# Row tiles 2 and 3 of batch 0 in the first 16 half steps of token block 0, and an earlier place for the next batch's bounds

## The chip, the cores and the metric

The kernel runs on one core of a Trainium2 chip. The metric is device time in microseconds (us), the median of the runs. Of three runs of the kernel before the median is 876.29 us (873.26 to 876.75). One further execution was profiled; every row below is from it.

## What is computed

The reference is a causal attention with a decay, followed by two feed-forward layers; only the core of it is shown.

```python
# q, k, v: 4 batches x 8 heads x 576 x 64, f: 4 x 8 x 576
scores = scale * q @ k.T
cum = cumsum(log(clip(f, 1e-4, 1)))
attn = softmax(where(causal, -1e9, scores + cum[:, None] - cum[None, :]))
x = (attn @ v)                      # as 2304 tokens x 512
h = x @ w_in                        # 512 -> 2048
x = (h * tanh(softplus(h))) @ w_out # 2048 -> 512
h = x @ w2_in                       # 512 -> 1024
s = h * softmax(h)
out = (layernorm(s) * g_ln) @ w2_out
```

## The kernel before, in words

Products run in halves: each operand is a 16-bit high part and a 16-bit low part, and three products (high-high, high-low, low-high) make one.

**Attention.** A batch has five row tiles of 128 query rows (tile 4 of batch 0 has 64), and a tile is worked in steps of 4, 2, 1, 1, 1 heads: 30 steps a batch, 120 in all (`seq`). A step runs through `step_s` (scores on PE into one of three PSUM tiles `sp`), `step_r` (row maximum on DVE, exponential on ACT into one of two buffers `p`), `step_h` (high part by a cast, low part on POOL, both in `ph`, two buffers; every second step of one head a transposing DMA `pT<-ph` leaves, two buffers `pT`), and `step_pv`, three steps behind (products with v on PE). `fin` closes a row tile: it scales the sums on DVE (`x`), splits them (`xh`, low part on POOL) and sends a transposing DMA into `xT`, the input of a token block of 256 tokens. Token block 1 needs row tiles 2 and 3 of batch 0.

**Feed-forward.** For each of nine token blocks, 16 ups (`up`, 12 matmuls each, L786) and 16 downs (`down`, L830) alternate, one of each in two half steps; between them lies the activation (`mish_a`, `mish_b`, `mish_c`, mostly on ACT). Attention steps are dealt to half steps by `att_slots`: `EB` = 190 half steps share the cost of all steps evenly, `lo` makes a block's steps be there by the end of the block before, `hi` holds them back.

**Weights.** While token block 0 runs, `w_in` and `w_out` are loaded in 1 MB parts (`wi_r`, `wo_r`, two buffers), unpacked on DVE (L133, L135, L137), bounded by a small product on PE (`gram`, L156, then `bound`), scaled to a high part on ACT (L198), and given a low part by products on PE (L205, L206) and a copy on ACT (L207).

**The next batch.** `ahead` is called with every step. It loads k and v of the next batch (`load_raw`, three buffers `raw` of 256 KB), squares them on ACT to bound them (`stats`, L330, buffer `x32`, which `fin` uses too), turns the bounds into scales (`scales`), and later loads q, k, v again, tile by tile, and splits them (`split_k`, `split_q`, `split_v`).

**What sets the order.** Every DMA goes out from one queue, SP's, in its order; an entry that waits holds all behind it. A scheduler lays the instructions of each engine out ahead of the run; its order starts from the program's and follows what it believes to be ready. So an edit in `ahead` or `att_slots` moves rows on every engine. A row below that names "issue" or an L number of a helper (L214 and the like) stands in a function called from those named here.

## Time and profile before

| | |
|---|---|
| median of 3 runs | 876.29 us |
| profiled execution, its own time | 874.98 us |
| span of its trace | 873.2 us |
| PE busy | 767.9 us (88%) |
| DVE, ACT, POOL busy | 593.5, 565.7, 392.1 us |
| chain that ended last, by engine | PE 42%, DVE 19%, DMA 16%, ACT 11% |

The time of the profiled execution is 1.8 us longer than its span; times of the trace count from the start of the span. PE is the busiest engine over the whole span; the rows further down show by stretches where it is not.

### The profile page before, as it was taken

What the parts mean: (1) busy time and instruction counts of PE and PEld (TensorE: products, weight loads), DVE (VectorE), ACT (ScalarE), POOL (GpSimd) and SP (SyncE); (2) the same over time, 40 slices, a digit from 0 to 9 for tenths busy, and PEclk for the clock granted to TensorE, in tenths of its full rate; (3) what the DMA queues carried; (4) which work ended last, traced back from release to release, by engine and by line L of the source; (5) the groups of instructions that cost most, each with busy time, mean ns of one, the idle gap of its engine ahead of it and who ended that gap; (6) DMA issues with size and microseconds to landing.
All of it is one profiled execution on the core that took longest, in us unless ns stands there. A gap on an engine that the chain in (4) does not pass through costs nothing.

```text
span 873.2 us, 16633 instructions
## 1 busy us (share of the span) xinstructions
PE 767.9 (88%) x6255; PEld 481.8 (55%) x6255; DVE 593.5 (68%) x1160; ACT 565.7 (65%) x1234; POOL 392.1 (45%) x321
## 2 busy tenths in 40 slices
PE   0469988779999988998889999986999999999997
PEld 0335555566667656566656666653555554444443
DVE  6797862757867989758897764689656454666451
ACT  5747766778768877778867667786965554333331
POOL 2232221645776677755587653226743132012110
PEclk9979999858999999999999999999999999999999
DMA  9998330788999789797897734662112523344453
GB/s 233 243 265 248 125 116 19 135 171 156 155 161 186 141 147 171 167 197 127 165 187 111 134 62 73 168 210 82 25 38 60 97 50 71 86 109 99 106 90 80
DMA packets 328573, 114.90 MB, mean 132 GB/s; under 512 B 317676, under 2 KB 317676, under 8 KB 328492
## 3 DMA queue, kind: packets, MB, share of 16 engines
q1 hardware_dynamic: 328492, 113.84, 63.5%
q8 instruction: 49, 0.80, 0.4%
q14 instruction: 32, 0.26, 0.1%
HBM read 46.59 MB, written 9.55 MB: 64 GB/s over the span
## 4 chain that ended last, share of the span: by engine, by line
PE 42%; DVE 19%; DMA 16%; ACT 11%; issue 6%; POOL 4%; SPq 1%; DVEq 0%; POOLq 0%; ACTq 0%
PE h L1027 10%; PE o L1067 10%; PE x L830 8%; PE h L786 7%; DMA pT<-ph 5%; DVE th L807 2%; POOL ph L518 2%; DVE ph L515 2%; DVE ta L803 2%; DMA wi_r<-in_moe_w_in_dram 2%; DMA rawk<-in_k_dram 1%; PE sp L205 1%; ACT p L479 1%; DMA wo_r<-in_moe_w_out_dram 1%; DMA w2i_r<-in_moe_w_in_dram 1%
## 5 line engine op out<-in xcount | busy, mean ns | idle before, releaser
L830 PE MATMUL x<-wout,gt 128*128 128x512 f16 x864 | 218.6, 386 | 18.6 <-ACT gt L812 8.5
L786 PE MATMUL h<-xT,win 128*128 128x256 f16 x1728 | 216.2, 274 | 1.5 <-DMA xT<-xh 1.5
L786 PEld LDWEIGHTS <-win 128*128 128x128 f16 x1728 | 166.1, 98 | 39.5 <-issue 2.8
L518 POOL TENSOR_TENSOR ph<-p,ph 128x512 f16<-128x512 f32 (+4 forms) x120 | 151.6, 1267 | 79.1 <-ACT ph L517 41.4
L813 POOL TENSOR_TENSOR gt<-th,gt 128x512 f16<-128x512 f32 x72 | 93.9, 1305 | 150.7 <-ACT gt L812 146.7
L830 PEld LDWEIGHTS <-gt 128*128 128x128 f16 x864 | 80.3, 99 | 99.3 <-ACT gt L812 13.5
L1055 POOL TENSOR_TENSOR z<-sl,z 128x1024 f16<-128x1024 f32 x18 | 38.7, 2150 | 138.2 <-DVE s2c L1034 111.3
L1027 PE MATMUL h<-w,x2T 128*128 128x512 f16 x432 | 98.4, 380 | 2.3 <-POOL w L221 1.2
L1067 PE MATMUL o<-wo,zT 128*128 128x512 f16 x432 | 96.5, 379 | 1.0 <-DMA zT<-z 1.0
L807 DVE SCALAR_TENSOR_TENSOR th<-ta,th 128x512 f32<-128x512 f32 x72 | 67.2, 934 | 40.7 <-ACT ta L806 40.4
L549 PE MATMUL pv<-vt,pT 128*128 128x64 f16 (+3 forms) x480 | 72.7, 205 | 23.3 <-DMA pT<-ph 20.1
L479 ACT ACTIVATE p<-sp,nm 64x64 f32<-64x64 f32 (+7 forms) x128 | 61.2, 484 | 34.1 <-DVE nm L477 21.6
L435 PE MATMUL sp<-kt,qa 128*128 128x128 f16 (+3 forms) x480 | 70.4, 221 | 12.8 <-ACT p L479 8.5
L436 PE MATMUL sp<-kt,qb 67*128 67x128 f16 (+3 forms) x480 | 72.1, 222 | 4.4 <-DMA kt<-dd 3.1
L812 ACT CAST gt<-th 128x512 f16<-128x512 f32 x72 | 44.4, 617 | 47.6 <-DVE th L807 46.1
L549 PEld LDWEIGHTS <-pT 128*128 128x128 f16 (+3 forms) x480 | 46.6, 103 | 48.3 <-DMA pT<-ph 31.5
L550 PE MATMUL pv<-vt,pT 128*128 128x64 f16 (+3 forms) x480 | 72.0, 201 | 0.0
L551 PE MATMUL pv<-vt,pT 128*128 128x64 f16 (+3 forms) x480 | 71.9, 201 | 0.0
L1027 PEld LDWEIGHTS <-x2T 128*128 128x128 f16 x432 | 42.3, 98 | 53.0 <-issue 3.1
L1067 PEld LDWEIGHTS <-zT 128*128 128x128 f16 x432 | 42.2, 98 | 52.1 <-DMA zT<-z 1.5
L1038 ACT ACTIVATE e<-h,s2c 128x1024 f32<-128x1024 f32 x18 | 21.7, 1204 | 68.0 <-DVE s2c L1036 68.0
L803 DVE TENSOR_SCALAR ta<-ta 128x512 f32<-128x512 f32 x72 | 49.9, 694 | 22.3 <-ACT ta L798 22.1
(231 smaller groups left out, 1496.8 us busy)
## 6 DMA issues: line engine op xcount, KB each, us to landing
wi_r<-in_moe_w_in_dram SPq DMA_DIRECT2D x8, 1024.0 KB
wo_r<-in_moe_w_out_dram SPq DMA_DIRECT2D x8, 1024.0 KB
rawk<-in_k_dram SPq DMA_DIRECT2D x25, 256.0 KB
rawv<-in_v_dram SPq DMA_DIRECT2D x25, 256.0 KB
x2d<-x2h SPq DMA_DIRECT2D x18, 256.0 KB
out_dram<-ro SPq DMA_DIRECT2D x18, 256.0 KB
w2i_r<-in_moe_w_in_dram SPq DMA_DIRECT2D x4, 1024.0 KB
w2o_r<-in_moe_w_out_dram SPq DMA_DIRECT2D x4, 1024.0 KB
```

The costliest lines, as they stand in the source:

```text
L435: nc.tensor.matmul(o, qa[:, h, r0:r1_], kc[:, h, a0:a1], start=True, stop=False)
L436: nc.tensor.matmul(o, qb_[:67, h, r0:r1_], kc[:67, H + h, a0:a1], start=False, stop=(c != i))
L518: nc.gpsimd.tensor_tensor(p4[:, :, 1], pv3, p4[:, :, 0], op=ALU.subtract)
L549: nc.tensor.matmul(o, pT[a0:a1, k, :m], vh, start=(c == 0), stop=False)
L550: nc.tensor.matmul(o, pT[a0:a1, k, :m], vl, start=False, stop=False)
L551: nc.tensor.matmul(o, pT[a0:a1, k + 1, :m], vh, start=False, stop=(c == i))
L786: nc.tensor.matmul(ph, win[:, (fi // 4) * NC1 + c, col:col + P], x[:, lx * NC1 + c, :], start=(m == 0), stop=(m == 3 * NC1 - 1))
L807: nc.vector.scalar_tensor_tensor(th, ta, 2.5, th, op0=ALU.subtract, op1=ALU.mult)
L813: nc.gpsimd.tensor_tensor(gt[:, 1], th, gt[:, 0], op=ALU.subtract)
L830: nc.tensor.matmul(o, gt[:, lg, n % 2, t * P:(t + 1) * P], wout[:, fi, lw * 512:(lw + 1) * 512], start=(first and m == 0), stop=(last and ...
L1027: nc.tensor.matmul(h[:, half * 512:(half + 1) * 512], x[:, lx * NC1 + c, :], self.w2[:, half * NC1 + c, lw * 512:(lw + 1) * 512], start=(n ...
L1067: nc.tensor.matmul(o, zT[:, lz * NF2 + c, :], self.wo[:, c, lw * 512:(lw + 1) * 512], start=(n == 0), stop=(n == 3 * NF2 - 1))
```

## The change

Two things are changed. In `att_slots`, while token block 0 runs, a second lower limit is added: from 9 steps at the start, one step is due in each of the first 16 half steps (`A0`), until row tiles 2 and 3 of batch 0 are in (16 steps; three more drain the pipeline). Before, the even share took 25 half steps to deal the same 16. After half step 15 no step is due until the even share has caught up in half step 26; from there on the two are the same.

In `ahead`, for every batch that has a next one, the loads of k and v stand beside tiles 2 to 4 and not 3 and 4 alone, their squares likewise, and the scales, the first q, k, v and its splits come one step earlier.

```diff
+A0 = 16
...
-        if b + 1 < B and i in (3, 4):
-            n = (i - 3) * H + h
-            if n in (0, 2, 4, 6, 8):
-                load_raw(b + 1, n // 2, "kv")
-            if n in (2, 4, 6, 8, 10):
-                stats(b + 1, n // 2 - 1, "kv")
-            if n == 11:
+        if b + 1 < B and i in (2, 3, 4):
+            n = (i - 2) * H + h
+            if n in (6, 8, 14, 15, 16):
+                load_raw(b + 1, (6, 8, 14, 15, 16).index(n), "kv")
+            if n in (8, 10, 15, 16, 17):
+                stats(b + 1, (8, 10, 15, 16, 17).index(n), "kv")
+            if n == 18:
                 scales(b + 1, "kv")
         if nb < B:
-            if h == (LD if ni else 12 - H) and nb > 0:
+            if h == (LD if ni else 3) and nb > 0:
                 load_raw(nb, ni, "qkv")
...
-            if h == (LD + 2 if ni else 5):
+            if h == (LD + 2 if ni else 4):
...
         lo = need[j + 1] + LAG if j + 1 < NBLK and r >= 2 * NF1 - ATE else 0
+        if j == 0:
+            lo = max(lo, n0 + LAG + min(need[1] - n0, (r + 1) * (need[1] - n0) // A0))
```

What this does to the order is seen at three places. In the rows, `pT_2_4` is the transpose of row tile 2, heads 4 and 5; the last number of a name only tells buffers apart. Line numbers of the kernel after are one higher here.

SP's queue around the last weight parts, before:

```order
L120 DMA wo_r_722<-in_moe_w_out_dram 128x2x512
L120 DMA wo_r_752<-in_moe_w_out_dram 128x2x512
L316 DMA rawk_2_1358<-in_k_dram 128x8x64
L120 DMA wi_r_804<-in_moe_w_in_dram 128x2x512
L120 DMA wi_r_817<-in_moe_w_in_dram 128x2x512
L523 DMA_TRANSPOSE pT_2_2_824<-ph_2_2_785 128x12x128
L120 DMA wo_r_933<-in_moe_w_out_dram 128x2x512
L120 DMA wo_r_946<-in_moe_w_out_dram 128x2x512
L523 DMA_TRANSPOSE pT_2_4_980<-ph_2_4_907 128x12x128
```

The same place, after:

```order
L121 DMA wo_r_722<-in_moe_w_out_dram 128x2x512
L121 DMA wo_r_767<-in_moe_w_out_dram 128x2x512
L317 DMA rawk_2_1391<-in_k_dram 128x8x64
L317 DMA rawv_2_1393<-in_v_dram 128x8x64
L317 DMA rawk_3_1452<-in_k_dram 128x8x64
L524 DMA_TRANSPOSE pT_2_2_802<-ph_2_2_731 128x12x128
L121 DMA wi_r_837<-in_moe_w_in_dram 128x2x512
L121 DMA wi_r_850<-in_moe_w_in_dram 128x2x512
L524 DMA_TRANSPOSE pT_2_4_938<-ph_2_4_855 128x12x128
L121 DMA wo_r_969<-in_moe_w_out_dram 128x2x512
L121 DMA wo_r_982<-in_moe_w_out_dram 128x2x512
```

`pT_2_2` has moved ahead of the last two parts of `w_in`, `pT_2_4` ahead of the last two of `w_out`, and two raw loads ahead of both.

SP's queue at the end of row tile 3, up to the transpose `xT` that token block 1 begins with, before:

```order
L523 DMA_TRANSPOSE pT_3_4_1460<-ph_3_4_1398 128x16x128
L316 DMA rawk_3_1477<-in_k_dram 128x8x64
L316 DMA rawv_3_1479<-in_v_dram 128x8x64
L523 DMA_TRANSPOSE pT_3_6_1573<-ph_3_6_1529 128x16x128
L316 DMA rawk_4_1615<-in_k_dram 128x8x64
L316 DMA rawv_4_1617<-in_v_dram 128x8x64
L523 DMA_TRANSPOSE pT_4_0_1702<-ph_4_0_1655 128x20x64
L316 DMA rawq_0_1858<-in_q_dram 64x8x64
L316 DMA rawk_0_1860<-in_k_dram 64x8x64
L523 DMA_TRANSPOSE pT_4_2_1835<-ph_4_2_1776 128x20x64
L316 DMA rawv_0_1862<-in_v_dram 64x8x64
L576 DMA_TRANSPOSE xT_1280<-xh_3_1758 128x8x128
```

The same place, after:

```order
L317 DMA rawk_0_1814<-in_k_dram 64x8x64
L317 DMA rawv_0_1816<-in_v_dram 64x8x64
L524 DMA_TRANSPOSE pT_3_0_1185<-ph_3_0_1152 128x16x128
L524 DMA_TRANSPOSE pT_3_2_1279<-ph_3_2_1244 128x16x128
L524 DMA_TRANSPOSE pT_3_4_1374<-ph_3_4_1324 128x16x128
L861 DMA x2d<-x2h_2165 128x1024
L524 DMA_TRANSPOSE pT_3_6_1468<-ph_3_6_1427 128x16x128
L861 DMA x2d<-x2h_2177 128x1024
L524 DMA_TRANSPOSE pT_4_0_1590<-ph_4_0_1552 128x20x64
L422 DMA_TRANSPOSE qa_0_1873<-qn_0_1870 128x8x64
L400 DMA_TRANSPOSE kt_0_1866<-kn_125 128x8x64
L577 DMA_TRANSPOSE xT_1234<-xh_3_1650 128x8x128
```

The raw loads are ahead of all four transposes of tile 3; `pT_4_2` has gone behind `xT`, and the next batch's `qa_0` and `kt_0` have come ahead of it.

ACT's order at tile 3's exponentials, before:

```order
L479 ACTIVATE p_1_129,rsum_3_1180<-sp_147,nm_3_5_1452 128x512
L517 CAST ph_3_4_1398<-p_1_129 128x4x128
L479 ACTIVATE p_0_128,rsum_3_1180<-sp_148,nm_3_6_1521 128x512
L858 ACTIVATE x2h_2165<-acc_1326,x2m_2159 128x512
L330 ACTIVATE jkk_1_1362,st_1248<-rawk_1_1244 128x512
L517 CAST ph_3_6_1529<-p_0_128 128x4x128
L330 ACTIVATE jkv_1_1364,st_1248<-rawv_1_1246 128x512
L479 ACTIVATE p_1_129,rsum_3_1180<-sp_146,nm_3_7_1565 128x512
```

ACT's order where six of these squares stand after, among the last weight copies (L199, L208):

```order
L480 ACTIVATE p_0_128,rsum_3_1148<-sp_148,nm_3_0_1149 128x512
L518 CAST ph_3_0_1152<-p_0_128 128x4x128
L331 ACTIVATE jkk_2_1456,st_1095<-rawk_2_1391 128x512
L331 ACTIVATE jkv_2_1458,st_1095<-rawv_2_1393 128x512
L331 ACTIVATE jkk_3_1516,st_1095<-rawk_3_1452 128x512
L199 ACTIVATE wout<-wout,wo_b 128x2x512
L799 ACTIVATE ta_1818<-h_12_1762,usc_0_79 128x512
L800 ACTIVATE th_1819<-h_12_1762 128x512
L331 ACTIVATE jkv_3_1518,st_1095<-rawv_3_1454 128x512
L805 ACTIVATE ta_1818<-ta_1818 128x512
L331 ACTIVATE jkk_4_1575,st_1095<-rawk_4_1512 128x512
```

The squares (`jkk`, `jkv`) have gone from among tile 3's exponentials to a place ahead of the last weight copies, and tile 3's first exponential stands ahead of them.

## Rows read from the trace of the kernel before

**Rows 1.** The page's granted clock, 40 slices of 21.8 us, in tenths.
```profile
PEclk9979999858999999999999999999999999999999
```

**Rows 2.** Busy time by stretches: length, then PE, PEld, DVE, ACT, POOL; clock, DMA, GB/s.
```profile
77.00:122.00 45.00, 43.18 (x325) 28.10 (x324) 30.09 (x63) 35.20 (x62) 11.47 (x9) 1.00 0.56 169
122.00:153.60 31.60, 25.09 (x168) 14.45 (x167) 14.98 (x32) 20.04 (x38) 5.10 (x5) 1.00 0.09 22
153.60:190.50 36.90, 25.93 (x341) 21.50 (x339) 23.80 (x62) 28.26 (x74) 21.13 (x18) 0.70 0.84 158
...
400.00:460.00 60.00, 50.55 (x533) 34.37 (x534) 55.38 (x96) 45.89 (x117) 40.02 (x34) 0.96 0.86 162
```

**Rows 3.** Timeline of PE, 156 to 206 us: start, duration, what, idle before it.
```profile
168.69 0.23 PE L549 MATMUL pv<-vt,pT 128*128 128x64 f16 x1 [1.20 <-DMA pT<-ph]
...
173.76 0.23 PE L549 MATMUL pv<-vt,pT 128*128 128x64 f16 x1 [2.06 <-DMA pT<-ph]
...
179.91 0.23 PE L549 MATMUL pv<-vt,pT 128*128 128x64 f16 x1 [2.85 <-DMA pT<-ph]
...
190.54 4.32 PE L786 MATMUL h<-xT,win 128*128 128x256 f16 x30
```

**Rows 4.** Chain that ended last, 0 to 260 us: start, duration, what.
```profile
114.99 6.70 DMA wo_r<-in_moe_w_out_dram
...
163.60 5.04 DMA pT<-ph
...
173.23 6.63 DMA pT<-ph
```

**Rows 5.** Timeline of SP's queue, 100 to 205 us; a duration includes its wait.
```profile
113.45 1.43 SPq L523 DMA_TRANSPOSE pT<-ph  x1
...
133.69 1.28 SPq L523 DMA_TRANSPOSE pT<-ph  x1
...
171.92 0.57 SPq L316 DMA_DIRECT2D rawk<-in_k_dram  x1
...
186.63 1.34 SPq L576 DMA_TRANSPOSE xT<-xh  x1
...
189.25 1.20 SPq L421 DMA_TRANSPOSE qa<-qn  x1
190.75 1.29 SPq L399 DMA_TRANSPOSE kt<-kn  x1
```

**Rows 6.** Timeline of ACT, 74 to 206 us.
```profile
80.48 0.72 ACT L216 ACTIVATE rawq<-rawq,scu 64x512 f32<-64x512 f32 x1 [1.98 <-DMA rawq<-in_q_dram]
...
110.89 0.57 ACT L479 ACTIVATE p<-sp,nm 128x384 f32<-128x384 f32 x1
...
152.99 0.64 ACT L207 ACTIVATE wout<-sp 128x512 f16<-128x512 f32 x1
...
156.79 0.69 ACT L479 ACTIVATE p<-sp,nm 128x512 f32<-128x512 f32 x1 [0.51 <-POOL ph L518]
157.38 0.19 ACT L479 ACTIVATION_READ_ACCUMULATOR p<-sp,nm 128x1 f32 x1
157.60 0.62 ACT L517 CAST ph<-p 128x512 f16<-128x512 f32 x1
```

**Rows 7.** The squares of the next batch (L330), 153 to 191 us: count, then min/median/max ns.
```profile
L330 ACT ACTIVATE jkk<-rawk x4: 617/621/638, 167.0 to 181.2; 128x512 f32<-128x512 f32 x4
```

**Rows 8.** Timeline of POOL, 140 to 206 us.
```profile
161.30 2.27 POOL L518 TENSOR_TENSOR ph<-p,ph 128x512 f16<-128x512 f32 x2 [1.85 <-ACT ph L517]
...
165.68 1.15 POOL L568 TENSOR_TENSOR xh<-x,xh 128x512 f16<-128x512 f32 x1
```

**Rows 9.** Timeline of DVE, 140 to 206 us.
```profile
183.49 0.67 DVE L564 TENSOR_TENSOR x<-pv,rr 128x512 f32<-128x512 f32 x1
...
184.20 0.43 DVE L567 CAST xh<-x 128x512 f16<-128x512 f32 x1
```

**Rows 10.** Waits of PE, 400 to 440 us: in total, times, longest.
```profile
PE pv L549 <- DMA pT<-ph: 5.0, 4, 1.8
```

## The prediction

> **What bounds the kernel now.** I read the page's clock row first, because a stretch in which PE starves shows there: the ninth slice (174.6 to 196.5 us) stands at 5 tenths, and no later one falls under 8 [rows 1]. The stretches around it say why [rows 2]. From 77 to 122 us PE is busy 43.2 of 45 us: token block 0 and the weight products fill it. From 122 to 153.6 us it is busy 25.1 of 31.6. From 153.6 to 190.5 us it is busy 25.9 of 36.9 at a granted clock of 0.70, that is, part of the time at 1.2 instead of 2.4 GHz, so even the busy time is inflated. That last stretch begins with the end of the last weight copy on ACT (152.99 + 0.64 [rows 6]) and ends with the first up of token block 1 at 190.54 [rows 3]. In it PE waits three times for a transpose of row tile 3 (1.20, 2.06 and 2.85 us, its products starting at 168.69, 173.76 and 179.91) [rows 3]. So a hole of 36.9 us lies in front of block 1, set by row tile 3's chain and not by PE's work. The change aims straight at it; it can give back some of the hole, and it can pay for that in the weight stage ahead of it.
>
> **The weight stage, 77 to 153.6 us.** PE does the same work ahead of row tile 3's first product with v: in the built order that product stands at the same place of PE's list in both kernels. Only waits can move the stage's end. There are three new ones.
>
> First, SP's queue. The last parts of w_out left at 114.99, right behind `pT_2_2` (113.45, 1.43 long) [rows 5], and took 6.70 us to land [rows 4]. `pT_2_2` was late because its second exponential ran only at 110.89 [rows 6]. Now it leaves earlier, but `pT_2_4` must leave ahead of w_out. Its second scores stand just behind the second gram product of w_in, which in the trace was over shortly before that exponential, 110.9. I add some 2 us because that part of w_in now leaves behind `pT_2_2`. From there: an exponential of 0.57, a cast and a low part (about 0.6 and 1.15 [rows 6, 8]), with other ACT work between, so `pT_2_4` leaves near 116 and w_out near 117.5: **2.5 us later**. Bounds: none, if it leaves by 113.5 as `pT_2_2` did, and 20 us, if it leaves at 133.69, where it does now [rows 5] (a rival below).
>
> Second, ACT. Eight squares of (0.62 + 0.19) us [rows 6, 7], 6.5 us in all, come ahead of the last weight copy. Two fall into an ACT idle of 1.98 us at 80.48 [rows 6]. Six, 4.9 us, fall into 122 to 153.6 us, where ACT is busy 20.0 of 31.6 us [rows 2]; cover is 11.5 us, but the rows are ahead of weight copies, so a late raw load would show in full. I take 0.5 us; bounds 0 and 4.9.
>
> Third, two row maxima on DVE among the unpacking of w_out (DVE busy 15.0 of 31.6 [rows 2]): no more than 1.2 us, and the unpacked parts wait for DVE; I take 0.5.
>
> Against these 3.5 us stand gains: PE idles 6.5 us in 122 to 153.6 [rows 2], and in the new order tile 2's and 3's products fill part of that while w_out is unpacked, with the bound of w_out read sooner behind them. I take 3.5 back. **Stage: 0, bounds -3 and +5.**
>
> **The hole.** I follow row tile 3 from the end t of the last weight copy. In the trace t is 153.6 and block 1 starts at t + 36.9. In the new order tile 3's first exponential is done before t, and the second stands two activations behind it: it ends at t + 2.0. Its cast waits for one more exponential (0.69 + 0.19) and takes about 0.6 [rows 6], its low part half of 2.27 [rows 8]: `pT_3_0` leaves at t + 4.6 and, at 5.04 or a little under for its landing [rows 4], lands at t + 9. From there the pace counts. In the trace it was 5.07 and 6.15 us between the starts of tile 3's last three products [rows 3]. In that time POOL also made xT_2's low part (1.15 us [rows 8]), ACT ran squares, and SP put two raw loads of 256 KB ahead of `pT_3_6` (171.92 on [rows 5]), which took 6.63 us to land instead of 5.04 [rows 4]. All of that is gone from the stretch. What is left for two transposes in flight: a cast 0.6, two low parts 2.3 and a landing near 5, 7.9 us for two, **4.0 a piece** (bounds: 2.3, two low parts on POOL alone, and 5.1, as now). So `pT_3_2` lands at t + 13, where the trace has 168.69, t + 15.1, and `pT_3_6` at t + 9 + 3 x 4.0 = t + 21, where it has 179.91, t + 26.3 [rows 3]. Then the division 0.67 and the cast 0.43 [rows 9], a low part 1.15 [rows 8] and small gaps, and PE's own 0.8 ahead of them: t + 24.5.
>
> Here SP takes something back. `xT_3` now stands behind `qa_0` and `kt_0` of the next batch, issues of 1.20 and 1.29 [rows 5], which wait for splits on DVE that stand just ahead of tile 3's cast. With them `xT_3` leaves near t + 25.3. It lands 3.9 us after its issue, as now (186.63 to 190.54 [rows 3, 5]): **t + 29**, against t + 36.9. That is 8 us less. Bounds: 3 (pace 5.1, and the two transposes ahead of `xT_3` cost another 1.5) and 12 (pace 3, nothing in front of `xT_3`).
>
> What is late next: one pair of tile 4's steps, which stood ahead of the first up, now stands behind it: 30 products with v and 8 score matmuls. The hole's 341 matmuls took 25.9 us at a clock of 0.70 [rows 2], 0.053 us each at full clock, so 2.0 us for the 38; some of it fills waits of block 1. **+1.5**, bounds 0 and 2.0.
>
> The clock in the hole: rows first. It was granted at 0.70 on the mean there, and the first 30 ups took 4.32 us [rows 2, 3]. The hole stays a run of short products with waits, so I leave it at the lower level for part of the time. The Trainium skill, page "TensorE: Matmul & The Clock Gate", section "What's actually happening", says that half clock is the state after idling and that activity lifts it; rows 1 and 2 agree. By that rule a hole dense enough for 2.4 GHz would return a part of the inflated busy time: a rival below.
>
> **The other two batch changes.** The loads, squares and scales of batches 2 and 3 move by the same table, beside feed-forward that keeps PE full. PE idles 9.4 of 60 us at 400 to 460 [rows 2], 5.0 of it for tile transposes [rows 10]. Raw loads leave that neighbourhood, as they do in the hole, but nothing else there changes. I take -1; bounds -4 and +3 (the squares now compete with activations while tile 2 runs).
>
> **Sum.** 0 - 8 + 1.5 - 1 = -7.5 us. Against the profiled execution's 874.98 this gives 867.5; the median of the runs lies 1.3 above that execution, so the forecast for the median lies between 867.5 and 868.8: **868.0**. After block 1's start everything is paced by half steps and PE, so what is won at its start I carry to the end.
>
> **The rivals.**
> 1. *The transposes ahead of the last weight parts hold them (slower).* Place: `pT_2_4` in SP's queue. If its exponentials come late, w_out waits with it; each us beyond 115 goes into t. It decides at about 122: there the loss equals the gain of 7.5. At 133.69, its time now, w_out lands 20 us later, some 8 of which PE could fill with work it has, and the total is 876 - 7.5 + 12 = 880.5 to 888. For it: SP's queue does not reorder, and ACT is busy. Against: its scores stand early in PE's order. Chance 0.12.
> 2. *The hole keeps its length.* The pace stays at 5.1, `xT_3` loses behind `qa_0` and `kt_0` what the raw loads had cost, and the later batches give nothing: gain 3 less 1.5, total 874.5. For: two of three waits are for transposes that remain. Against: the 6.63 us landing with raw loads in front. Chance 0.24.
> 3. *More comes back.* The pace falls to 3, the clock rises earlier in the hole (25.9 busy us at 0.70 would be 18.1 at full clock, most of the difference on no path), and the later changes give their 4: 859 to 862. By the Trainium skill ("DMA: Bandwidth & Descriptors", section "Latency and other measured facts") a transpose runs at 261 GB/s, so the 512 KB of `pT_3` would take 2.0 us, an estimate; the trace's 5.04 from issue to landing is used instead. Chance 0.12.
> 4. *The forecast*, 864 to 872. Chance 0.52.
>
> **How the numbers follow.** The range runs from rival 3's lower end to just short of rival 1's: 859 to 878, leaving out about 0.15. A measurement of this kernel can tell about 0.5%, 4.4 us, from no change: below 871.9 is faster, above 880.7 slower. Faster gets the forecast's 0.52 and rival 3's 0.12, a little of it passed to the middle: 0.63. Slower gets 0.10 of rival 1. The rest, 0.27, lies between.
>
> **What would show it.** Right: the last w_out parts leave SP near 117, the last L207 copy ends within 3 us of 153.6, no square stands between tile 3's exponentials, tile 3's products with v start 4 us apart, and block 1's first up follows the last weight copy by 29 us. Wrong: w_out leaving after 122, or that last distance staying above 33; or, with the hole shorter as told, a total that does not follow, which would mean that something later than block 1's start sets the end.

## The result, and the profile after

The kernel after takes 864.15 us (median; 863.13 to 868.76) against 876.15 us of the kernel before in the same comparison: ratio 0.9873, 95% interval 0.9843 to 0.9903, that is 1.3% faster. The forecast was 868.0 with a range of 859 to 878, "faster" the likeliest sign. Number and sign held; the sections below show that the reason I gave for them mostly did not.

The execution of the kernel after that was profiled took 868.76 us (span 867.0), the longest of its runs, so its trace shows 6.2 us of the gain and not 12. Line numbers of the kernel after are one higher than before.

Its clock row, to be held against [rows 1]: the ninth slice is now 6 tenths instead of 5, with 9 on either side of it where 8 stood.

```profile
PEclk9979999969999999999999999998999999999999
```

Busy time by stretches, as in [rows 2] (length, then PE, PEld, DVE, ACT, POOL; clock, DMA, GB/s). The second stretch ends with the last weight copy, the third with the first up of block 1:

```profile
77.00:122.00 45.00, 42.45 (x316) 27.08 (x316) 31.18 (x62) 37.05 (x70) 12.67 (x10) 1.00 0.56 161
122.00:155.70 33.70, 29.17 (x217) 18.24 (x214) 17.37 (x39) 24.27 (x50) 12.54 (x7) 0.95 0.45 104
155.70:186.20 30.50, 19.73 (x269) 15.32 (x267) 21.76 (x58) 21.56 (x53) 14.38 (x12) 0.79 0.63 118
400.00:460.00 60.00, 51.90 (x551) 36.03 (x551) 51.57 (x89) 46.24 (x123) 41.56 (x37) 1.00 0.90 166
```

SP's queue, as in [rows 5]: the transpose of row tile 2 (`pT_2_4`) with the last two parts of `w_out` right behind it, the last transpose of tile 3, then `qa_0`, `kt_0` and `xT_3`.

```profile
116.67 1.28 SPq L524 DMA_TRANSPOSE pT<-ph  x1
118.04 1.52 SPq L121 DMA_DIRECT2D wo_r<-in_moe_w_out_dram  x2
...
172.55 1.91 SPq L524 DMA_TRANSPOSE pT<-ph  x1
...
180.43 1.20 SPq L422 DMA_TRANSPOSE qa<-qn  x1
181.67 1.26 SPq L400 DMA_TRANSPOSE kt<-kn  x1
182.99 1.30 SPq L577 DMA_TRANSPOSE xT<-xh  x1
```

PE's timeline, as in [rows 3]: the waits for tile 3's transposes.

```profile
164.44 0.20 PE L550 MATMUL pv<-vt,pT 128*128 128x64 f16 x1 [0.60 <-DMA pT<-ph]
168.31 0.20 PE L550 MATMUL pv<-vt,pT 128*128 128x64 f16 x1 [0.45 <-DMA pT<-ph]
171.97 0.20 PE L550 MATMUL pv<-vt,pT 128*128 128x64 f16 x1 [2.20 <-DMA pT<-ph]
177.35 0.23 PE L550 MATMUL pv<-vt,pT 128*128 128x64 f16 x1 [1.96 <-DMA pT<-ph]
```

Block 1's first up stands at 186.26 in that timeline, where before it stood at 190.54 [rows 3].

ACT's timeline, as in [rows 6]: tile 3's first exponential, the first of the six squares that now stand in the weight stage, the last weight copy, which ends at 155.70 (153.63 before), and tile 3's second exponential.

```profile
137.85 0.68 ACT L480 ACTIVATE p<-sp,nm 128x512 f32<-128x512 f32 x1
...
141.40 0.63 ACT L331 ACTIVATE jkk<-rawk 128x512 f32<-128x512 f32 x1 [2.12 <-POOL xh L569]
...
155.08 0.62 ACT L208 ACTIVATE wout<-sp 128x512 f16<-128x512 f32 x1
...
156.87 0.67 ACT L480 ACTIVATE p<-sp,nm 128x512 f32<-128x512 f32 x1
```

At first sight this is the prediction come true: from the last weight copy to block 1's first up it is 30.6 us instead of 36.9, and 29 was said. But block 1 starts only 4.3 us earlier, and the columns of the table above say more. In the hole PE is idle 30.50 - 19.73 = 10.8 us; before it was 36.90 - 25.93 = 11.0 [rows 2]. The hole became shorter because 6.2 us of PE's busy time left it (269 matmuls stand in it, not 341), not because PE waits less in it.

**Where the gain lies.** To compare kernels whose pieces stand in another order, both need a point at which the same work is done. I take the second cast `x2h` of block 5 on ACT, which follows that block's last downs (552.33 before, 546.72 after): in the trace of every kernel of this study 4621 matmuls start ahead of it, the last of attention among them. Two points ahead of it divide the stretch, though there the kernels have not done quite the same work: block 1's first up, and the same cast of block 3 (431.71 and 419.56). Stretches of the kernel before, columns as above:

```profile
77.00:190.50 113.50, 94.21 (x831) 64.05 (x830) 68.87 (x155) 83.50 (x171) 37.69 (x31) 0.90 0.52 124
190.50:431.70 241.20, 219.91 (x2371) 157.09 (x2368) 188.95 (x342) 190.18 (x479) 159.04 (x139) 0.97 0.89 161
431.70:552.30 120.60, 113.38 (x1158) 78.89 (x1159) 87.20 (x145) 85.13 (x191) 76.75 (x69) 0.97 0.64 112
```

and of the kernel after:

```profile
77.00:186.20 109.20, 91.35 (x793) 60.64 (x793) 70.30 (x158) 82.88 (x171) 39.59 (x29) 0.93 0.55 131
186.20:419.60 233.40, 219.04 (x2379) 157.79 (x2379) 185.65 (x333) 183.67 (x458) 155.87 (x138) 0.97 0.91 162
419.60:546.70 127.10, 115.32 (x1188) 80.80 (x1186) 88.01 (x151) 90.17 (x213) 79.45 (x72) 0.99 0.63 112
```

Length less busy time is PE's idle time: 19.3, 21.3 and 7.2 us before, 17.9, 14.4 and 11.8 after. So up to block 1's start 1.4 us of idle time are gained; from there to block 3's end 6.9; in blocks 4 and 5 4.6 are lost. PE's busy time in all three falls by 1.8. Together that is the 5.6 us by which block 5 ends earlier; the rest of the span adds 0.6. Of the 3.7 us of idle time that are gained, 1.4 lie ahead of block 1's start and a net 2.3 behind it; in a second profile of the kernel after (below) it is 1.5 and 4.2. So the larger part of the idle time gained stands **behind** block 1's start, the stretch for which the prediction had -1 and "what is won at its start I carry to the end", and ahead of it there is little of the 8 us forecast.

### The profile page after: what moved, and what is told of

It reads as the page before. It is cut to its first block, busy times and chain, and to the rows that moved or that the text cites. A ratio compares the mean times of both kernels' runs of the same rounds, so it can differ in the third digit from the quotient of the medians.

```text
span 867.0 us, 16642 instructions
## 1 busy us (share of the span) xinstructions
PE 766.6 (88%) x6255; PEld 481.0 (55%) x6255; DVE 594.2 (69%) x1160; ACT 563.7 (65%) x1234; POOL 394.2 (45%) x321
## 4 chain that ended last, share of the span: by engine, by line
PE 40%; DVE 19%; DMA 16%; ACT 9%; issue 9%; POOL 6%; SPq 1%; DVEq 0%; POOLq 0%; ACTq 0%
PE h L1030 10%; PE o L1070 10%; PE x L831 7%; PE h L787 7%; DMA pT<-ph 5%; POOL ph L519 3%; DMA wo_r<-in_moe_w_out_dram 2%; DVE ta L804 2%; POOL gt L814 2%; ACT p L480 2%; DMA xT<-xh 1%; DMA w2i_r<-in_moe_w_in_dram 1%; DVE th L808 1%; DVE vt L215 1%; DVE ph L516 1%
## 5 line engine op out<-in xcount | busy, mean ns | idle before, releaser
L787 PE MATMUL h<-xT,win 128*128 128x256 f16 x1728 | 221.0, 279 | 1.8 <-DMA xT<-xh 1.8
L519 POOL TENSOR_TENSOR ph<-p,ph 128x512 f16<-128x512 f32 (+4 forms) x120 | 155.4, 1301 | 92.0 <-ACT ph L518 42.3
L787 PEld LDWEIGHTS <-win 128*128 128x128 f16 x1728 | 170.0, 100 | 45.1 <-issue 5.5
L550 PE MATMUL pv<-vt,pT 128*128 128x64 f16 (+3 forms) x480 | 68.6, 200 | 23.3 <-DMA pT<-ph 22.9
L808 DVE SCALAR_TENSOR_TENSOR th<-ta,th 128x512 f32<-128x512 f32 x72 | 64.6, 898 | 30.5 <-ACT ta L807 28.0
L480 ACT ACTIVATE p<-sp,nm 64x64 f32<-64x64 f32 (+7 forms) x128 | 61.2, 484 | 27.3 <-DVE nm L478 12.9
L804 DVE TENSOR_SCALAR ta<-ta 128x512 f32<-128x512 f32 x72 | 53.7, 746 | 23.5 <-ACT ta L799 23.2
L550 PEld LDWEIGHTS <-pT 128*128 128x128 f16 (+3 forms) x480 | 44.3, 100 | 45.8 <-DMA pT<-ph 29.6
L552 PE MATMUL pv<-vt,pT 128*128 128x64 f16 (+3 forms) x480 | 67.8, 195 | 0.0
L551 PE MATMUL pv<-vt,pT 128*128 128x64 f16 (+3 forms) x480 | 67.8, 195 | 0.0
L805 ACT ACTIVATE ta<-ta 128x512 f32<-128x512 f32 x72 | 45.3, 631 | 34.0 <-DVE ta L804 33.8
```

Of the source, the lines that this page charges most:

```text
L480: nc.scalar.activation(pv[:m, g * (i + 1) * P + off:g * (i + 1) * P + end], s3[:, g, off:end], AF.Exp, bias=nm[:m, g:g + 1], accum_out=rs[ ...
L519: nc.gpsimd.tensor_tensor(p4[:, :, 1], pv3, p4[:, :, 0], op=ALU.subtract)
L550: nc.tensor.matmul(o, pT[a0:a1, k, :m], vh, start=(c == 0), stop=False)
L787: nc.tensor.matmul(ph, win[:, (fi // 4) * NC1 + c, col:col + P], x[:, lx * NC1 + c, :], start=(m == 0), stop=(m == 3 * NC1 - 1))
L804: nc.vector.tensor_scalar(ta, ta, E20, 1.0, op0=ALU.min, op1=ALU.add)
L808: nc.vector.scalar_tensor_tensor(th, ta, 2.5, th, op0=ALU.subtract, op1=ALU.mult)
```

## The experiments

Two theories stood at the start. Mine: the limit in `att_slots` and the moved loads and squares both shorten the hole ahead of block 1, and that is the gain. The rival: one part does it all, and the other does nothing or costs. Every ratio is to the kernel before, run in turns with it on the same chip. The kernels ran in three groups of four, close to the order in which they are told; only the kernel with the places of batches 1 and 2 and the limit ran with the last group. Each diff shows what sets the kernel apart: from the kernel before for the limit alone and for the two without bounds, from the kernel after for the others, unless the text says otherwise.

### The kernel after once more, and its two parts apart

The kernel after, unchanged.

> The changed kernel itself, to have a second profile. My theory: about 4 to 5 us are won by the first up of token block 1 (hole from the last weight copy to that up 30 to 31 us, against 36.9 before) and the rest later, since the profiled execution of it had 186.3 us for that up and 868.8 in all. If more than 8 of the 12 us are won by that up in this profile, the first profile was the odd one and the later batches give nothing. Time: 862 to 867 us.

Measured: 866.21 us, ratio 0.9906 (0.9885 to 0.9927). Beside 0.9873 (0.9843 to 0.9903) this says how far two comparisons of the same kernel lie apart: 0.3%, their intervals overlapping. Smaller differences between two of the kernels below are not read. The expected time held.

The limit alone:

```diff
+        if j == 0:
+            lo = max(lo, n0 + LAG + min(need[1] - n0, (r + 1) * (need[1] - n0) // A0))
```

> Only the 16 half steps (att_slots), ahead as before. My theory (hole): raw loads stand ahead of tile 3's transposes here too, so most of the hole's gain comes, about 4 us, and the later batches' part is missing: 868 to 872. Rival (the bounds' place does it): the squares and raw loads still disturb, at most 2 us of gain, 874 or more.

Measured: 871.14 us, ratio 0.9964 (0.9946 to 0.9982). The limit alone is worth some 0.4%, as I expected in total. Its hole is as short as that of the kernel after: the last weight copy ends at 155.96, and block 1 starts 31.6 us later. Its first up, on PE's timeline:

```profile
187.60 5.02 PE L787 MATMUL h<-xT,win 128*128 128x256 f16 x23 [3.62 <-DMA xT<-xh]
```

PE waits 3.62 us for `xT_3` here. So the hole is 5.3 us shorter, and the total falls by about half of that. And the limit alone already takes the loads and squares of the bounds out of the hole: of the eight squares that stood in it before (167.04 to 181.95 on ACT's timeline) seven now run ahead of the last weight copy and one as it ends, and of the loads one is left, at 156.59, ahead of all of tile 3's transposes. The last two squares:

```profile
153.72 0.65 ACT L331 ACTIVATE jkk<-rawk 128x512 f32<-128x512 f32 x1
...
155.82 0.65 ACT L331 ACTIVATE jkv<-rawv 128x512 f32<-128x512 f32 x1
```

The new places in `ahead` alone, for all batches, without the limit:

```diff
-        if j == 0:
-            lo = max(lo, n0 + LAG + min(need[1] - n0, (r + 1) * (need[1] - n0) // A0))
```

> Only the new place of loads, squares and scales (ahead), pacing as before. My theory: part of the hole's gain, since squares and some raw loads leave tile 3's stretch, but that stretch starts no earlier: 869 to 874. Rival (the pacing does it): 875 or more. Rival (the bounds do it all): 866 or less.

Measured: 863.79 us, ratio 0.9878 (0.9859 to 0.9896). My expectation missed, the rival's held: the places alone give the whole gain. And they give it with a long hole: the last weight copy ends at 152.88, block 1's first up stands at 187.82, 34.9 us later, 2 less than before. Six squares (166.34 to 177.86) and three loads of the bounds (169.47 to 171.32) still stand in it: without the limit the new places in the program do not take them out.

### The batches apart

The places of batch 1 alone, with the limit. `ahead` is called with the step of the batch ahead, so b == 0 is where batch 1 is prepared.

```diff
+        if b == 0:
+            if b + 1 < B and i in (2, 3, 4):
...
+        else:
+            if b + 1 < B and i in (3, 4):
...
```

> The changed kernel with ahead's new places for batch 0 alone; batches 1 and 2 place their loads as before. The forecast gave the later batches 1 us: 865 to 866. If the later batches carry what the first profile leaves over after block 1's start (about 8 of 12 us), 870 to 872.

Measured: 865.30 us, ratio 0.9896 (0.9871 to 0.9922), the same as the kernel after in that group and the time that I expected. The same without the limit:

> Only the new places of loads, squares, scales and first splits of batch 1 (beside batch 0's tiles); batches 2 and 3 as before, no second lower limit. In the run with all batches moved and no limit, the time was 863.8 us against 873.5 before, and PE idle between 77 us and the last downs of block 5 fell from 47.8 to 40.3 us. Theory: the gain lies in batch 0, since batches 2 and 3 took as much back as they gave when the limit was there (865.3 with batch 1 alone, 866.2 with all): 862 to 866, first exponential after the last weight copy and block 1's first up as in that run (last copy near 153, first up near 188). Rival: half the gain was the later batches': 868 to 870.

Measured: 867.35 us, ratio 0.9905 (0.9881 to 0.9930): between the two expected ranges, with the last weight copy at 151.13 and the first up at 185.97, both 2 us ahead of what I had expected. So the limit does nothing beside batch 1's new places (0.9896 against 0.9905), and the later batches' places, on the whole, do nothing beside the limit (0.9906 against 0.9896).

The places of batches 1 and 2, batch 3 as before, without the limit (the condition is b <= 1):

> New places for batches 1 and 2, batch 3 as before, no second lower limit. Theory: in the changed kernel PE idles 11.8 us between the last downs of blocks 3 and 5 (419.6 to 546.7) where the kernel before idles 7.2 (431.7 to 552.3) and the kernel with batch 1 alone 6.1; that stretch holds the work of batch 3 and the loads for it, so with batch 3's old places the gain up to block 3 stays and the loss goes: 857 to 861. Rival: those idle times are a matter of where the pieces fall in each order and do not add: within 2 us of the run with all batches moved, 862 to 866.

Measured: 860.55 us, ratio 0.9824 (0.9797 to 0.9850): the lowest time of the study, below the kernel with all batches moved (0.9878, intervals apart), and below both measurements of the kernel after (0.9873 and 0.9906; the first one's interval overlaps). Its stretches to the same three points:

```profile
77.00:185.10 108.10, 91.84 (x802) 61.52 (x802) 70.39 (x155) 83.23 (x170) 35.99 (x31) 0.91 0.53 129
185.10:418.30 233.20, 219.24 (x2407) 157.63 (x2407) 185.68 (x343) 188.05 (x478) 158.51 (x140) 0.98 0.92 164
418.30:537.10 118.80, 111.72 (x1152) 78.25 (x1151) 83.29 (x143) 84.93 (x190) 75.11 (x69) 0.99 0.66 118
```

The idle times are 16.3, 14.0 and 7.1 us: the middle is that of the kernel after, and the 11.8 of its last stretch are back at 7.1, as before. That is what I expected of this run. But the step from it to "batch 3's early loads cost this" is not safe: the kernel with all batches moved and no limit idles 6.6 us in its last stretch (416.8 to 540.6), also with batch 3's early loads.

The same with the limit:

> The changed kernel with batch 3's places as before: the second lower limit and the new places for batches 1 and 2. Beside the run with the same places and without the limit (ratio 0.9824) it tells what the limit does there. Theory: the limit moves work across block 1's start and gives nothing of its own: ratio 0.980 to 0.986, some 858 to 863 us. Rival: it costs the 3 to 4 us that lie between the run of the changed kernel (0.9906 in one comparison) and the same without the limit (0.9878): ratio 0.986 to 0.990.

Measured: 860.96 us, ratio 0.9833 (0.9806 to 0.9860). As expected, the limit moves no total here either. With and without it, batch 2's places lower the ratio by 0.6 to 0.8 per cent (0.9896 to 0.9833, 0.9905 to 0.9824) and batch 3's take most of that back (to 0.9873 and 0.9906, to 0.9878).

### Two queue terms of the prediction

The prediction priced `pT_2_4` ahead of the last `w_out` parts at 2.5 us. Here those parts are no longer tied behind it:

```diff
-        group=4, after=lambda: pend.get("pt"), gram=grams)
+        group=4, after=None, gram=grams)
```

> The changed kernel, with the issue of the w_out parts no longer tied behind the transposes of row tile 2: the last two parts leave ahead of pT_2_4. Theory: that tie costs the limit its gain; with it gone the last parts leave near 112.7, as in the run without the limit (112.66), and not at 118; the last weight copy ends at 152 to 154 and not at 155.7 to 156.2, and the total is 861 to 864. Rival: the 3 us are covered (PE has products of tiles 2 and 3 to do meanwhile), or pT_2_4 behind 1 MB parts loses as much: 865 to 868.

Measured: 865.70 us, ratio 0.9889 (0.9863 to 0.9916), the same as the kernel after. SP's queue and, from ACT's timeline, the last weight copy:

```profile
103.11 3.49 SPq L121 DMA_DIRECT2D wo_r<-in_moe_w_out_dram  x2
...
117.41 1.44 SPq L524 DMA_TRANSPOSE pT<-ph  x1
```

```profile
157.24 0.61 ACT L208 ACTIVATE wout<-sp 128x512 f16<-128x512 f32 x1
```

The first of the two parts leaves 15 us earlier than in the kernel after, and the last weight copy ends 2.1 us **later** (157.85). So an earlier departure of `w_out` did not bring the end of the weight stage forward. It is not a test of that wait alone: PE's order in the two traces is the same only for the first 41 matmuls. The time fits the rival's 865 to 868; whether the wait is covered or the new order takes back what it gave is not shown.

The other term was `xT_3` behind `qa_0` and `kt_0`. Here `kt_0` (`i` in the first lines) and `qa_0` may leave only behind it:

```diff
+        if b == 1 and c == 0:
+            later(tc, i, pend["xt"])
...
+        if b == 1 and c == 0:
+            later(tc, pend["qt"], pend["xt"])
```

> The changed kernel, with qa_0 and kt_0 of batch 1 issued behind xT_3, not ahead of it. Theory: xT_3 leaves 2 us earlier after the last weight copy (near +25 and not +27.3), block 1's first up follows at +28 to +29, and the total falls by 1 to 2 us, to 863 to 865. Rival: qa_0 and kt_0 are then late for batch 1's first scores, or what starts earlier is only moved: 865 to 869.

Measured: 872.06 us, ratio 0.9955 (0.9937 to 0.9973), slower than the kernel after by 0.5 to 0.8 per cent, its interval apart from both of that kernel's, and above both expected ranges. SP's queue:

```profile
182.32 1.23 SPq L581 DMA_TRANSPOSE xT<-xh  x1
183.60 1.28 SPq L400 DMA_TRANSPOSE kt<-kn  x1
184.92 1.27 SPq L424 DMA_TRANSPOSE qa<-qn  x1
```

`xT_3` leaves 27.0 us after the last weight copy (155.31), where it left 27.3 after it in the kernel after: nothing won. What it waits for is its own low part, on POOL's timeline of this kernel:

```profile
181.14 1.15 POOL L573 TENSOR_TENSOR xh<-x,xh 128x512 f16<-128x512 f32 x1 [1.97 <-DVE xh L572]
```

which ends at 182.29. The two us that I expected from the queue (the prediction had put 0.8 on it) lie on DVE. In the kernel after DVE's timeline reads:

```profile
178.92 0.69 DVE L565 TENSOR_TENSOR x<-pv,rr 128x512 f32<-128x512 f32 x1 [1.15 <-PE pv L552]
179.64 0.75 DVE L215 SCALAR_TENSOR_TENSOR qn<-rawq,scu,qn 64x512 f16<-64x512 f32 x1
180.31 0.75 DVE L215 SCALAR_TENSOR_TENSOR kn<-rawk,scu,kn 64x512 f16<-64x512 f32 x1
181.10 0.43 DVE L568 CAST xh<-x 128x512 f16<-128x512 f32 x1
```

The splits of the next batch's `q` and `k` stand between tile 3's division and its cast and hold the cast for 1.4 us, and for as long in this kernel, where they stand at the same place (179.19 to 180.61, the cast at 180.64). That they stand there the prediction had seen, but it took their cost to be that of the queue. Why this kernel is slower is not shown here, only where: PE's order is that of the kernel after for the first 1057 matmuls, down to block 1's start, and the last of these starts at 185.1 us against 185.6. What is lost is lost behind them, where the orders differ.

### The suspected work taken away

By now the places of batch 1 looked like the gain, and the loads and squares in the hole like what the old places cost. The direct test is a kernel before that doesn't have them: no loads and no squares for the bounds of batch 1, a constant in their place.

```diff
-                load_raw(b + 1, n // 2, "kv")
+                if b + 1 in BND:
+                    load_raw(b + 1, n // 2, "kv")
...
+        if b not in BND:
+            return
```

> The kernel before, without the ten loads and ten squares that bound k and v of batch 1 (a constant stands for the bound, so that part of the computation is left out). Theory: the loads between the transposes of row tile 3 and the squares on ACT between its exponentials are what the hole ahead of token block 1 costs, and moving them (867 us with the new places for batch 1 alone) gave back nearly all of it: 863 to 867 here, with the transposes of tile 3 landing 4 us apart. Rival: the gain of the moved kernels comes from the other order that the scheduler makes, or from the scales and splits one step earlier: above 870.

Measured: 868.56 us, ratio 0.9917 (0.9894 to 0.9941). Above the 863 to 867 of the theory, though below the rival's 870: taking the work away gives about what the new places gave (0.9905). But those places had not taken the work out of the hole, as my expectation supposed. The first and the last of six squares in the kernel with batch 1's places and no limit, whose first up stands at 185.97:

```profile
164.58 0.62 ACT L331 ACTIVATE jkk<-rawk 128x512 f32<-128x512 f32 x1
...
175.97 0.63 ACT L331 ACTIVATE jkv<-rawv 128x512 f32<-128x512 f32 x1
```

Nor is the hole cured without the work: the last weight copy ends at 152.39, the first up stands at 186.19, 33.8 us later, with no load and no square in between. And a transpose still takes long. SP issued seven transposes `pT` from 150 to 190 us in the next kernel, which has no such loads at all; the view of their line gives this time from issue to landing (least, median, most):

```profile
DMA to landing us min/median/max: 4.3/4.6/4.9
```

The trace holds the landing of only two of the seven, 4.3 and 4.9 us. They agree with the kernel after, where the last transpose of tile 3 leaves at 172.55 and PE, waiting for it, starts at 177.35. So the 5.04 us of [rows 4] owes little to the loads (the 6.63 behind two of them may owe more), and the estimate of 2.0 us that the prediction drew from the Trainium skill ("DMA: Bandwidth & Descriptors", "Latency and other measured facts") is not what this transpose does here, with the queue clear of loads either.

Without the bounds of batches 1, 2 and 3:

> The kernel before, without the loads and squares that bound batches 1, 2 and 3 (constants stand for the bounds). It shows the most that any place for them can give. Theory: the waits for transposes between 281 and 432 us (9.4 us before, 2.9 with batches 1 and 2 moved) are the bounds' doing too: 852 to 860, and the kernel with batches 1 and 2 moved (860.6, ratio 0.982) has most of it. Rival: in the later batches PE's other work hides them: within 3 us of the run that leaves out batch 1's alone.

Measured: 877.24 us, ratio 1.0020 (1.0003 to 1.0038). Thirty loads and thirty squares fewer, and the kernel is no faster; it is 1.0% slower than the one that leaves out batch 1's alone. Both sides of my expectation missed. Its three stretches:

```profile
77.00:185.60 108.60, 94.14 (x795) 63.47 (x793) 70.06 (x151) 76.87 (x148) 33.68 (x28) 0.88 0.42 107
185.60:426.30 240.70, 217.05 (x2349) 156.49 (x2347) 185.74 (x335) 172.53 (x418) 156.91 (x138) 0.96 0.76 137
426.30:555.10 128.80, 120.64 (x1217) 84.52 (x1218) 89.75 (x153) 92.36 (x217) 79.93 (x72) 0.96 0.66 114
```

Idle times are 14.5, 23.7 and 8.2 us. Up to block 1's start it is among the best of the study; in the middle stretch it is the worst. What PE waits for there is told by its waits from 185.6 to 426.3 us (in total, times, longest):

```profile
PE pv L552 <- DMA pT<-ph: 16.7, 14, 4.4
```

against the same row of the kernel before, from 190.5 to 431.7:

```profile
PE pv L549 <- DMA pT<-ph: 10.6, 12, 2.6
```

and of the kernel after, from 186.2 to 419.6:

```profile
PE pv L550 <- DMA pT<-ph: 5.8, 6, 1.8
```

So PE waits longer for transposes in this stretch, with fewer transfers on the queue. The two kernels without bounds have the same order of PE for the first 1559 matmuls and start the last of these at 243.3 us (batch 1's left out) and 242.8 (all left out); the 9 us by which the second ends block 5 later (555.1 against 546.3) arise behind that. So the amount of this work does not order the times here. What else differs between these kernels is the order that the scheduler lays out, on every engine and down to block 5: of PE's 2400 products with v and scores, 1248 start ahead of block 3's first up in the kernel before and in the kernel after, 1202 with the places of all batches and no limit, 1272 without any bounds.

### Loads and squares alone

Last, the new places of batch 1's loads and squares alone; scales, first `q`, `k`, `v` and their splits as before, no limit. The diff is against the kernel with all of batch 1's places and no limit, and lies under `b == 0`.

```diff
-                if n == 18:
+                if n == 19:
                     scales(b + 1, "kv")
-                if h == (LD if ni else 3) and nb > 0:
+                if h == (LD if ni else 12 - H) and nb > 0:
-                if h == (LD + 2 if ni else 4):
+                if h == (LD + 2 if ni else 5):
```

> Of the new places only those of the loads and squares of batch 1; its scales, its first q, k, v and their splits stay where they were, as do batches 2 and 3, and there is no second lower limit. Theory: the loads and squares are the gain of 8 us that batch 1's places gave together: 866 to 869. Rival: the splits one step earlier are needed too, since the first kt and qa then no longer come behind tile 3's last division: 871 to 875.

Measured: 861.12 us, ratio 0.9842 (0.9814 to 0.9871): more than all of batch 1's places together (0.9905, intervals apart), and below my 866 to 869. And in this kernel, one of the three fastest of the study, the squares stand **in** the hole, as in every kernel with new places and no limit. The first and the last of six on ACT's timeline:

```profile
164.60 0.62 ACT L331 ACTIVATE jkk<-rawk 128x512 f32<-128x512 f32 x1
...
176.13 0.64 ACT L331 ACTIVATE jkv<-rawv 128x512 f32<-128x512 f32 x1
```

and block 1's first up stands where it stood before (190.54 [rows 3]), 39.3 us after the last weight copy (151.17):

```profile
190.47 5.60 PE L807 MATMUL h<-xT,win 128*128 128x256 f16 x36
```

The hole is longer than in the kernel before, with the squares in it, and the kernel is 14 us faster. Its stretches:

```profile
77.00:190.50 113.50, 95.83 (x840) 65.35 (x840) 73.73 (x160) 86.69 (x182) 37.62 (x32) 0.89 0.54 129
190.50:423.80 233.30, 218.24 (x2395) 157.78 (x2395) 184.85 (x338) 185.13 (x470) 157.51 (x139) 0.98 0.92 165
423.80:539.30 115.50, 111.12 (x1127) 76.95 (x1125) 80.72 (x143) 84.70 (x191) 76.12 (x69) 0.99 0.65 114
```

Idle times are 17.7, 15.1 and 4.4: 1.6, 6.2 and 2.8 less than before. In this kernel at least, the hole ahead of block 1 is not where the gain comes from.

### All of them side by side

Worked out from each trace as above; "hole" is the time from the last weight copy to block 1's first up, "squares in it" those for the bounds of batch 1 that still run behind that copy, idle times are PE's in the three stretches, busy time is PE's in all three. Times of stretches are from one profiled execution each.

| kernel | limit | ratio | block 1 starts | hole | squares in it | idle 1, 2, 3 | busy |
|---|---|---|---|---|---|---|---|
| before | - | 1 | 190.5 | 36.9 | 8 | 19.3, 21.3, 7.2 | 427.5 |
| after | + | 0.9873 | 186.3 | 30.6 | 0 | 17.9, 14.4, 11.8 | 425.7 |
| after, again | + | 0.9906 | 187.1 | 30.9 | 0 | 17.8, 14.1, 10.2 | 425.0 |
| limit alone | + | 0.9964 | 187.6 | 31.6 | 1 | 20.0, 18.5, 7.7 | 426.5 |
| places, all batches | - | 0.9878 | 187.8 | 34.9 | 6 | 17.0, 16.7, 6.6 | 423.3 |
| places, batch 1 | - | 0.9905 | 186.0 | 34.8 | 6 | 16.0, 16.5, 7.2 | 427.2 |
| the same | + | 0.9896 | 185.4 | 30.4 | 0 | 16.4, 17.7, 6.1 | 428.0 |
| places, batches 1 and 2 | - | 0.9824 | 185.1 | 34.5 | 6 | 16.3, 14.0, 7.1 | 422.8 |
| the same | + | 0.9833 | 187.4 | 30.7 | 0 | 18.4, 15.2, 5.9 | 425.8 |
| loads and squares of batch 1 | - | 0.9842 | 190.5 | 39.3 | 6 | 17.7, 15.1, 4.4 | 425.2 |
| no bounds of batch 1 | - | 0.9917 | 186.2 | 33.8 | 0 | 14.5, 19.8, 6.0 | 429.1 |
| no bounds at all | - | 1.0020 | 185.6 | 34.5 | 0 | 14.5, 23.7, 8.2 | 431.8 |
| w_out not tied | + | 0.9889 | 190.1 | 32.3 | 1 | 17.9, 9.8, 8.4 | 427.8 |
| xT_3 first | + | 0.9955 | 186.3 | 31.0 | 0 | 17.1, 17.8, 8.0 | 430.2 |

Neither the start of block 1 nor the length of the hole orders the times: the kernel that starts block 1 at 185.6 is the slowest, one that starts it at 190.5 among the fastest. Every kernel with the limit in this table (marked +) has the short hole, 30.4 to 32.3 us; every one without it has 33.8 or more. So the hole's length goes with the limit, and in good part because the hole starts later: the last weight copy ends at 155.0 to 157.8 us with the limit and at 150.6 to 153.6 without. The limit also takes the squares out of the hole; the new places without it leave six in. Yet the places without the limit have the low ratios (0.9824 to 0.9905), and the limit alone has 0.9964. So clearing the hole is not what the gain comes from. The totals differ most behind it, in the middle stretch (9.8 to 23.7 us idle) and in PE's busy time (422.8 to 431.8).

## Why the prediction was right in number and wrong in reason

**Right.** `pT_2_4` leaves at 116.67 (116 said) and `w_out` at 118.04 (117.5). No square stands behind tile 3's second exponential (156.87); the six stand between it and the first (137.85), which runs that far ahead of it. Tile 3's products with v start at t + 8.7, 12.6, 16.3 and 21.7 (t = 155.70); t + 9, 13 and 21 were said for the first, second and last. The pace is 3.87 and 3.66 us, then 5.38 for the last, against 4.0. Block 1's first up comes at t + 30.6, within the bounds of the 29.

**The weight stage** ended 2.1 us later, not at 0 but inside its bounds. That the wait for `w_out` did it is not borne out: with `w_out` some 15 us earlier, if in another order, the stage ended later still. A wait that I had not priced stands there: ACT idles 2.12 us ahead of the first moved square, whose buffer `x32` is also `fin`'s and was being read by POOL for tile 2's `xh`. Whether that wait is the cause was not tried.

**The step that failed** is the -8 for the hole. I took its length as if it were PE's loss. Of the 36.9 us only 11.0 were idle; 25.9 were work that has to be done somewhere. The kernel after has a hole 6.4 us shorter and 10.8 us of idle time in it: 4.1 us more work is done in the weight stage (29.17 against 25.09 us of PE from 122 on), and the 38 matmuls of tile 4's pair stand behind the first up. The carry-over term counted the pair, at 1.5, but nothing counted that PE's time in the weight stage had to be lengthened by the rest. Block 1 starts 4.3 us earlier: 1.4 us of this is idle time and 2.9 busy time, some 2.0 of it the 38 matmuls that come later now, by the prediction's own price for them. The step should have been that term: -1.4 in the trace in place of -8 + 1.5 + 0.

**The causes named for the hole** fell with it. Loads and squares between tile 3's steps make at most some 3 of its 36.9 us (33.8 without batch 1's), and taking them out of the hole, as the limit alone does, is worth 0.4%, while the kernels that keep six squares in it gain 0.9 to 1.8%. The transposes' landing, where the trace tells it, is 4.3 and 4.9 us with no such load on the queue. `qa_0` and `kt_0` ahead of `xT_3` cost nothing that shows; the splits on DVE ahead of tile 3's cast do.

**The step "carried to the end"** failed as well, and in the useful direction. The later blocks were forecast at -1; they gave 6.9 us of idle time up to block 3's end and took back 4.6 in blocks 4 and 5, and over all three stretches 1.8 us of busy time came off, for which the prediction had no term. It is luck that -8 in the wrong place and this make about the same total, 6.2 us in the trace and 12.0 between the medians against 7.5; the rivals were priced on the hole too and are no nearer to what happened.

**What stays open.** Which row of the new order saves the 6 to 7 us between block 1's start and block 3's end is not settled. Shown is that most of the gain comes with the places in `ahead` (0.9878 without the limit) and little with the limit (0.9964 alone), and that it does not come from a hole free of loads and squares. What the loads and squares themselves cost is not separated: without batch 1's the kernel is 0.8% faster, without all of them it is no faster at all, and each of these edits re-deals the order too. That the order decides is argued by exclusion and not shown; no run holds the order fixed. Of the 6.9 us of idle time, 4.8 are waits for transposes (10.6 and 5.8 above). These go along with the total in some kernels (16.7 us without bounds, 10.6 before, 5.8 after), but not in all: with batch 1's loads and squares alone moved they are 10.4 us in a kernel that is 1.6% faster. That several kernels of nearly the same content lie anywhere from 0.9824 to 0.9917 also says that a single edit's share of the gain can't be read off to better than half a per cent here.

**A version that beats both.** The places for batches 1 and 2 with batch 3 as before, without the limit, at 860.55 us (ratio 0.9824); the limit can be added without effect (0.9833).

## What to carry to other kernels

A new place in the program is not yet a new place in the run: here the places alone left the squares in the hole, and the limit alone took them out, which only the trace of each part showed. The length of a stretch up to a row of the program is no loss; PE's idle time is, and it is compared only up to a point at which both kernels have done the same work. Before an edit that moves work out of the way is priced, the work should be left out once: if that makes nothing faster, the amount of that work is not the cost, with the caution that leaving it out changes the order too. Where a scheduler lays out the order, an edit in one place re-deals the work for hundreds of microseconds behind it, and sometimes ahead of it; several neighbouring variants are worth running, since here they differed by more than the change itself was worth.

## What the runs showed of the hardware

The two transposes of row tiles 3 and 4 whose landing the trace tells took 4.3 and 4.9 us from their issue with no load for the bounds on the queue, hardly less than the 5.04 of [rows 4].

PE's granted clock in the hole was 0.70 before, 0.79 after, and 0.62 in the kernel without bounds (151.1 to 185.6): means over stretches in which both levels, 1.2 and 2.4 GHz, occur. PE's busy time up to the end of block 5 differed by 9 us between kernels that have the same products, 4621 matmuls up to there in their traces: 422.8 with batches 1 and 2 moved, 431.8 without bounds, with a mean granted clock of 0.974 and 0.957 over their spans. The idle times of these two differ by as much (37.3 and 46.3). So half of the 18 us between them lies in PE's busy time, which I had not expected to move at all behind the hole. The other kernels go the same way: the mean clock of the five with the least busy time is 0.970 to 0.974 and once 0.966, that of the five with the most 0.957 to 0.966. The Trainium skill, page "TensorE: Matmul & The Clock Gate", section "What's actually happening", on which the prediction drew, has the lower clock follow idling; here the kernel with more idle time is the one with the lower clock. The sum of idle time does not order the clock of all kernels, though: with `w_out` not tied PE idles 36.1 us at a mean clock of 0.964, with the limit alone 46.2 us at 0.971.
